# Routed attention and a gated convolution FFN on one core: query pieces of 512 and 256 in place of two of 384, f32 weight loads, and a new order

## The chip, the cores and the metric

The kernel runs on one core of a Trainium2 chip. Its engines work from queues of their own and meet at semaphores: TensorE (PE in the profile; its weight loads are listed as PEld), VectorE (DVE), ScalarE (ACT), GpSimd (POOL) and SyncE (SP), which here only issues transfers (DMA). The metric is device time of one execution in microseconds, the median of several runs.

## The reference

Attention over 4 batches, 8 heads, 768 tokens and head size 64, in which a query sees only the keys that are nearest to the same one of 16 centroids, and then a feed-forward network with a 3-tap depthwise convolution as its gate:

```python
q_assign = np.argmax(np.einsum('bhsd,hcd->bhsc', q_n, c_n), axis=-1)
k_assign = np.argmax(np.einsum('bhsd,hcd->bhsc', k_n, c_n), axis=-1)
mask = q_assign[:, :, :, None] == k_assign[:, :, None, :]
scores = scale * np.matmul(q, k.transpose(0, 1, 3, 2))
scores = np.where(mask, scores, -1000000000.0)
attn = np.exp(scores - np.max(scores, axis=-1, keepdims=True))
attn = attn / (np.sum(attn, axis=-1, keepdims=True) + 1e-09)
x = np.matmul(attn, v)      # heads side by side: (4, 768, 512)

h = np.maximum(x @ w_in, 0.0)               # 512 -> 1024
conv_out = sum(conv_w[k] * hp[:, k:k + S, :] for k in range(3))   # hp: h padded by one
out = h * (1 / (1 + np.exp(-conv_out))) @ w_out                   # 1024 -> 512
```

## The kernel before

Heads are taken two at a time: 16 pairs g, four for each batch. For each pair, queries and keys come in by DMA (`load_q`, `load_k`, or `load_blocks`), are turned so that the head's 64 features lie along the partitions, and are cast to f16 into `ext`. Pairs 0 to 5 are loaded as rows of 64 values and turned by PE (`transposes`, L303, then `chunk_copy`, L316 and L318). Pairs 6 to 15, listed in `BLOCKS`, are loaded in pieces of 32 values by eight transfers a pair (`load_blocks`, L284) and turned by DVE in blocks (`turn_blocks`, L312). Centroid similarities (`assign`, L345), an argmax on DVE (`argmax`, L371 to L402), a turn on PE (`turn`, L407) and a copy (`spk`) give three more rows, 64 to 66, that carry the routing into the product as a bias; one transfer puts them in place (`bias_rows`, L415), and another shifts the second head's rows to partition 0 (`shift_pair`, L332). The pool of loaded pairs, `qk_in`, has three buffers, so pair g+3 can be loaded when pair g has been turned.

Attention runs in 32 slots t, eight for a batch: first the four pairs with queries 0 to 383, then the four with queries 384 to 767. A slot has six steps. In each, PE makes two 128x384 score tiles into one of two PSUM tiles `sc` (`scores`, L440), ACT takes the exponential of both at once (`exps`, L452, 768 columns), and PE multiplies with the values (`values`, L463). A column of ones beside the values gives the sum, by which DVE divides (`normalize`, L476 and L477). The result `x` is turned into `xT`, by PE for slots 0 to 3 and 28 to 31 and by a transposing transfer for the others (`xT_transfer`, L499).

The feed-forward network runs in eight units for each batch: half of the tokens, two blocks of 128 channels. A unit takes eight projection matmuls (`ffn_in`, L518), two relus (`relu`, L531 on ACT or L533 on DVE), three tap steps for each block on DVE (`tap`, L552 and L554; for five units of the last batch PE does the convolution, `conv`, L560), a tanh on ACT (`tanh`, L581) and a gate on DVE (`gate`, L589). Output matmuls (`ffn_out`, L601) gather all units of a batch, and `evac` (L614, L616) and `store` (L619) bring them out. Two or three columns at the seam of the token halves pass through POOL (`carry`, L540 and L542).

Weights are loaded by DMAs that POOL issues and that turn f32 into f16 on the way (`load_weights`, L627 and L632).

Nothing is scheduled by the compiler. `PLAN`, a string of some 1,700 tokens, gives the order in which every step is written; each engine and each DMA queue carries out its own steps in that order. `S.1.0@0` is scores of slot 1, step 0, into `sc` 0; `E`, `V` and `N` are exponential, values and normalising; `T.3.0@3` is the turning of chunk 0 of pair 3 into PSUM bank 3; `LQ`, `LK` and `LV` are loads, `CX` is the row shift, `BX` the bias rows.

Of the kernel before, what the change touches and what calls it, by code (L numbers as in the profile page):

```python
# [20 lines left out]
NHP = 3  # L21
NBH = 1
BLOCKS = (6, 7, 8, 9, 10, 11, 12, 13, 14, 15)

# [822 lines left out]
```

## Time and profile before

| | us |
|---|---|
| median of 3 runs (272.72, 272.73, 276.73) | 272.73 |
| profiled execution, its own time | 274.73 |
| its span, first to last instruction | 272.9 |
| first exponential begins | 15.76 |
| exponentials of slots 8, 16 and 24 begin | 78.78, 139.29, 195.38 |
| last exponential begins | 242.83 |

An idle engine is told with the event that ended its wait. Two views of who waited for whom matter here. The first is for ACT's exponentials and for PE's scores (engine and line, then what it waited for, us in total, times, longest):

```
ACT attn L452 <- PE sc L440: 16.5, 30, 1.9
PE sc L440 <- ACT attn L452: 2.7, 7, 1.2
DVE hg L589 <- ACT th L581: 5.9, 8, 1.7
```

The second is for SP's queue, whose issues stand in one line:

```
SPq L415 <- ACT attn L452: 16.3, 8, 5.1
SPq L332 <- POOL ext L318: 11.6, 3, 7.4
SPq L499 <- DVE cnv L554: 11.0, 5, 5.4
```

A matmul's end is modelled, so a PE that is listed as busy need not run at its peak. The granted clock is given as a share of full speed.

### The profile page before, as it was taken

Reading aid. Unit: us, or ns where it says so; the run is one execution under the profiler, and the core shown is the slowest. Engines: PE = TensorE matmul, PEld = TensorE weight load, DVE = VectorE, ACT = ScalarE, POOL = GpSimd, SP = SyncE. Lnnn points to the kernel's source line nnn. Section 1 sums busy time; section 2 is a strip of 40 time slices with the busy share of each in tenths; the row PEclk is TensorE's granted clock in tenths of the full one; section 3 lists DMA queues with packets and bytes.
Section 4 is the critical chain, followed back from the end, with each engine's and each line's share of the span. In section 5 each row is a group of like instructions: output and inputs, shape, how many; then the busy total and the mean of one; then the engine's idle time right before and its main releaser. Section 6 shows DMA issues by size and latency. Waiting matters only on the chain.

```text
span 272.9 us, 6362 instructions
## 1 busy us (share of the span) xinstructions
PE 243.0 (89%) x2414; PEld 149.0 (55%) x2414; DVE 218.6 (80%) x456; ACT 214.2 (78%) x338; POOL 83.2 (30%) x158
## 2 busy tenths in 40 slices
...
PEclk9999555799999799779999999999999999999999
...
GB/s 185 225 224 218 124 151 175 142 188 109 161 150 158 141 172 148 99 127 73 197 115 121 156 46 147 143 114 52 116 171 4 34 24 123 40 79 0 77 4 154
DMA packets 116458, 33.32 MB, mean 122 GB/s; under 512 B 109320, under 2 KB 111880, under 8 KB 116427
## 3 DMA queue, kind: packets, MB, share of 16 engines
...
q10 hardware_dynamic: 928, 0.23, 0.4%
q14 instruction: 12, 0.10, 0.1%
...
## 4 chain that ended last, share of the span: by engine, by line
DVE 35%; PE 29%; DMA 12%; ACT 9%; issue 5%; SPq 5%; POOL 2%; ACTq 0%; DVEq 0%; POOLq 0%
DVE cnv L554 12%; PE sc L440 9%; DMA qk_in<-in_q_dram 6%; ACT attn L452 5%; DVE qkT L312 4%; DVE hg L589 4%; PE flex L463 4%; PE flex L601 4%; SPq L284 3%; PE sc L601 3%; DVE cnv L552 3%; DMA ext<-ext 2%; ACT th L581 2%; PE flex L303 2%; DVE x L477 2%
## 5 line engine op out<-in xcount | busy, mean ns | idle before, releaser
L452 ACT ACTIVATE attn<-sc 128x768 f16<-128x768 f32 x192 | 148.9, 815 | 17.8 <-PE sc L440 16.5
L440 PE MATMUL sc<-ext 67*128 67x384 f16 x384 | 98.7, 350 | 5.1 <-ACT attn L452 2.7
L554 DVE SCALAR_TENSOR_TENSOR cnv<-hpad,cwcol,cnv 128x382 f16<-128x382 f16 (+1 forms) x108 | 68.2, 641 | 2.5
L463 PEld LDWEIGHTS <-attn 128*128 128x128 f16 x1152 | 52.8, 101 | 21.0 <-issue 7.2
L463 PE MATMUL flex<-v,attn 128*128 128x65 f16 x1152 | 56.9, 198 | 1.9 <-ACT attn L452 1.2
L440 PEld LDWEIGHTS <-ext 67*128 67x128 f16 x384 | 34.5, 103 | 31.1 <-issue 10.6
L318 POOL CAST ext<-qkT 128x768 f16<-128x768 f32 (+1 forms) x28 | 26.5, 960 | 68.1 <-PE sc L440 21.1
L601 PE MATMUL flex<-w_out,hg 128*128 128x512 f16 x152 | 44.1, 389 | 3.3 <-DVE hg L589 1.6
L518 PE MATMUL flex<-xT,w_in 128*128 128x384 f16 x228 | 45.7, 330 | 0.6 <-DVE sim L371 0.6
L589 DVE SCALAR_TENSOR_TENSOR hg<-th,hpad 128x764 f16<-128x764 f32 (+3 forms) x37 | 32.0, 870 | 6.0 <-ACT th L581 5.9
L518 PEld LDWEIGHTS <-w_in 128*128 128x128 f16 x256 | 24.5, 98 | 18.0 <-issue 2.6
L601 PEld LDWEIGHTS <-hg 128*128 128x128 f16 x192 | 17.5, 99 | 22.7 <-issue 7.5
L581 ACT ACTIVATE th<-cnv 128x764 f32<-128x764 f16 (+1 forms) x27 | 22.9, 851 | 7.5 <-DVE cnv L554 7.1
L531 ACT ACTIVATE hpad<-flex 128x384 f16<-128x384 f32 x47 | 22.7, 505 | 3.7 <-PE flex L518 3.6
L312 DVE STREAM_TRANSPOSE qkT<-qk_in 128x384 f32<-128x384 f32 x40 | 21.4, 558 | 1.3 <-DMA qk_in<-in_k_dram 0.8
L552 DVE TENSOR_SCALAR cnv<-hpad,cwcol 128x382 f16<-128x382 f16 (+1 forms) x54 | 18.6, 353 | 1.3 <-ACT hpad L531 1.2
L722 POOL TENSOR_SCALAR taps<-id,cwcol 128x128 f16<-128x128 f16 x24 | 19.4, 821 | 0.0
L477 DVE TENSOR_TENSOR x<-flex,rec 128x384 f16<-128x384 f32 x32 | 17.8, 557 | 1.1
L318 POOL CAST v<-v_in 128x768 f16<-128x768 f32 x14 | 12.4, 891 | 16.0 <-DMA v_in<-in_v_dram 11.0
L303 PE MATMUL flex<-id,qk_in 128*128 128x128 f32 x72 | 14.0, 347 | 2.5 <-ACT cP L681 1.0
L540 POOL COPY hf<-hpad 128x6 f16<-128x6 f16 x16 | 4.8, 303 | 32.6 <-ACT hpad L531 26.6
L542 POOL COPY hpad<-hf 128x6 f16<-128x6 f16 x16 | 5.5, 346 | 28.4 <-DVE hg L589 27.9
...
## 6 DMA issues: line engine op xcount, KB each, us to landing
...
```

Source lines behind the costliest of these rows:

```text
L312: nc.vector.transpose(turned(g)[:, 384 * i : 384 * (i + 1)], src)
L318: (nc.vector if name == "d" else nc.gpsimd).tensor_copy(out=to, in_=src)
L440: nc.tensor.matmul(sc[at][:, n, 0:HS], lhsT=ext_b[g % NE][0:KR, h, 1, P * (kt + n) : P * (kt + n + 1)], rhs=ext_b[g % NE][0:KR, h, 0, HS * ...
L452: nc.scalar.activation(attn[t, i // 3][:, kt : kt + 2, :], sc[at][:, :, 0:HS], AF.Exp, scale=0.125)
L463: nc.tensor.matmul(avp(at)[:, 3 * h + jq, 0 : D + 1], lhsT=attn[t, h][:, kt, P * jq : P * (jq + 1)], rhs=v16_b[g % NE][:, h, kt, 0 : D + 1 ...
L477: nc.vector.tensor_tensor(out=x16[t].rearrange("p jq (h d) -> p h jq d", h=2), in0=av[:, :, 0:D].rearrange("p (h jq) d -> p h jq d", h=2), ...
L518: nc.tensor.matmul(bank[at][:, 0:HS], lhsT=w_in16[:, r, 2 * u + f, :], rhs=xT[:, b % 2, r, HS * a : HS * (a + 1)], start=(r == 0), stop=(r ...
L552: nc.vector.tensor_scalar(out=cnv, in0=src, scalar1=w, scalar2=None, op0=ALU.mult)
L554: nc.vector.scalar_tensor_tensor(out=cnv, in0=src, scalar=w, in1=cnv, op0=ALU.mult, op1=ALU.add)
L581: nc.scalar.activation(to, pre, AF.Tanh, scale=0.5)
L589: nc.vector.scalar_tensor_tensor(out=hg_b[b][:, 2 * u + fs.start : 2 * u + fs.stop, LO[a] : LO[a] + N], in0=th_t[n][:, fs, 0:N], scalar=1. ...
L601: nc.tensor.matmul(bank[at][:, 0:Dm], lhsT=hg_b[b][:, fb, P * tq : P * (tq + 1)], rhs=w_out16[:, fb, :], start=(fb == 0), stop=(fb == NFB ...
```

## The change

Queries of a pair are now taken as 512 and 256. The first four slots of a batch have 512 queries, with two 128x512 tiles to a step, and the last four have 256, with four 128x256 tiles. So a slot has six or three steps of 1024 columns, with one exponential each. Each head of a 512-slot has a PSUM bank of its own for its values and is normalised by itself; the reciprocal is a step of its own (`P`).

The feed-forward network follows: for each batch four units of 512 tokens and two channel blocks, and two units of 256 tokens and four channel blocks. Units 19, 22 and 23 are convolved by PE.

Pairs 6 and 7 leave `BLOCKS` and are loaded and turned as pairs 0 to 5 are. For the pairs that stay, the keys are put in another order when they are cast, so that every pair's values can be loaded by one transfer with runs of 1536 bytes; POOL reads the keys with a step of six for that.

Weights come as f32 over SP into the buffers of `hg` and `th` and are cast by POOL (four), ACT (two) and DVE (two). Convolution weights come as 24 rows of 128 and are turned at once. Twelve matmuls of zeros (`_k`) are put in at the beginning, and `PLAN` is new throughout.

```diff
-BLOCKS = (6, 7, 8, 9, 10, 11, 12, 13, 14, 15)
+BLOCKS = (8, 9, 10, 11, 12, 13, 14, 15)
...
-    "LQ.0.0 _zero _cent _hz.1 _v.0 _cT _v.3 _v.4 _pk.3 LK.0.0 La.0.1 _id LQ.1.0 _n0 _pk.2 _id16 _pk.0 LV.0 "
+    "LQ.0.0 _cent _io _cT _v.1 _id La.0.1 LK.0.0 _zero _pk.1 _id16 _n0 LQ.0.1 _v.0 _v.4 _v.2 _k.0@0 _pk.0 "
...
-    HS = S // 2
-    NU = 2 * NPR
+    NU = NPR + NPR // 2
+    QN = (4 * P, S - 4 * P)
+    Q0 = (0, QN[0])
+    NF = (2, 4)
+    CUT = QN[0] - 2
...
     def cast_pair(name, g, x):
-        copy(name[2:], ext_b[g % NE][:, 0, x], qkT[g][:, x, :])
+        to, src = ext_b[g % NE][:, 0, x], qkT[g][:, x, :]
+        if x and g in BLOCKS:
+            to, src = to.rearrange("p (j t) -> p j t", j=J), src.rearrange("p (t j) -> p j t", j=J)
+        copy(name[2:], to, src)
...
+    def key_tiles(a, i):
+        n = 2 if a == 0 else 4
+        return [divmod(n * i + m, J) for m in range(n)]
...
     def exps(t, i, at):
+        a = slot(t)[1]
         if i % 3 == 0:
-            attn[t, i // 3] = rot.tile([P, J, HS], F16, name="attn", tag="attn", bufs=NAT)
-        kt = 2 * (i % 3)
-        nc.scalar.activation(attn[t, i // 3][:, kt : kt + 2, :], sc[at][:, :, 0:HS], AF.Exp, scale=0.125)
+            attn[t, i // 3] = rot.tile([P, J * QN[0]], F16, name="attn", tag="attn", bufs=NAT)
+        to = attn[t, i // 3][:, 1024 * (i % 3) : 1024 * (i % 3 + 1)]
+        nc.scalar.activation(to, sc[at].rearrange("p n s -> p (n s)"), AF.Exp, scale=0.125)
...
+    def reciprocals(t, h):
+        rec_t[t, h] = rot.tile([P, 4, 1], F32, name="rec", tag="rec")
+        nc.vector.reciprocal(out=rec_t[t, h][:], in_=avp(av_at[t, h])[:, :, D : D + 1])
+    def normalize(t, h):
+        av, rec = avp(av_at[t, h]), rec_t.pop((t, h))
+        if t not in x16:
+            x16[t] = rot.tile([P, 4, P], F16, name="x16", tag="x16", bufs=NX)
+        if slot(t)[1] == 0:
+            to, src, by = x16[t][:, :, D * h : D * (h + 1)], av[:, :, 0:D], rec[:].to_broadcast((P, 4, D))
+        else:
+            to = x16[t][:, 0:2].rearrange("p jq (h d) -> p h jq d", h=2)
...
+        nc.vector.tensor_tensor(out=to, in0=src, in1=by, op=ALU.mult)
...
     def unit(n):
-        return n // NU, n % NU // NPR, n % NPR
+        b, m = divmod(n, NU)
+        a = int(m >= NPR)
+        return b, a, m - NPR * a, NF[a] * (m - NPR * a)
...
-    def load_weights(i):
+    def load_weights(i, queue=nc.sync):
+        if i < 6:
+            if i % 3 == 0:
+                staged = rot.tile([P, NFB, S], F16, name="hg", tag="hg").bitcast(F32)
...
+        else:
+            staged = rot.tile([P, TH], F32, name="th", tag="th")
+            to = stage[i] = staged[:, 0:Dff]
         if i < R:
-            nc.gpsimd.dma_start(
-                w_in16[:, i].rearrange("p fb f -> p (fb f)"), moe_w_in[P * i : P * (i + 1), :]
-            )
+            queue.dma_start(to, moe_w_in[P * i : P * (i + 1), :])
...
+    def cast_weights(name, i):
+        if i < R:
+            to = w_in16[:, i].rearrange("p fb f -> p (fb f)")
+        else:
+            to = w_out16[:, 2 * (i - R) : 2 * (i - R) + 2].rearrange("p f d -> p (f d)")
+        copy(name[2:], to, stage.pop(i))
```

How the steps now stand is seen on three engines. In these rows a name is followed by the number of its buffer: `flex_68` to `flex_71` are PSUM banks 0 to 3, `sc_66` and `sc_67` the two score tiles, `ext_90` to `ext_92` the cast pairs 0 to 2. A row ends with its output's shape.

PE at its start, before:

```order
L670 MATMUL flex_68<-id_72,cn 128x128
L303 MATMUL flex_68<-id_72,qk_in 128x128 x3
L303 MATMUL flex_69<-id_72,qk_in 128x128 x3
L345 MATMUL flex_69<-qkT,cH 32x192 x4
L303 MATMUL flex_69<-id_72,qk_in 128x128 x3
```

and now, from the eleventh of the twelve matmuls of zeros on (`cn` are the centroids, `qk_in` the first pair):

```order
L686 LDWEIGHTS id_73
L686 MATMUL flex_68<-zero,id_73 128x384
L709 MATMUL flex_69<-id_72,cn 128x128
L297 MATMUL flex_70<-id_72,qk_in 128x128 x3
L297 MATMUL flex_71<-id_72,qk_in 128x128 x3
```

Eleven such matmuls stand ahead of the centroids, and the first two chunks of the pair no longer use the centroids' bank.

ACT from the copies of pair 1's chunks on, before:

```order
L316 ACTIVATE qkT<-flex_71 128x512
L316 ACTIVATE qkT<-flex_70 128x512
L452 ACTIVATE attn<-sc_66 128x768
L452 ACTIVATE attn<-sc_67 128x768
L316 ACTIVATE ext_90<-flex_71 3x384
L452 ACTIVATE attn<-sc_66 128x768
L316 ACTIVATE qkT<-flex_70 128x512
L452 ACTIVATE attn<-sc_67 128x768
```

and now:

```order
L310 ACTIVATE qkT<-flex_68 128x512
L310 ACTIVATE ext_91<-qkT 128x768 x2
L310 ACTIVATE ext_90<-flex_71 3x384
L459 ACTIVATE attn<-sc_66 128x1024
L459 ACTIVATE attn<-sc_67 128x1024
L310 ACTIVATE qkT<-flex_71 128x512
L459 ACTIVATE attn<-sc_66 128x1024
L459 ACTIVATE attn<-sc_67 128x1024
```

Both casts of pair 1 (`ext_91`) and the bias rows of pair 0's second head now stand ahead of the first exponential.

SP's queue from the key loads of pair 3 on, before:

```order
L278 DMA qk_in<-in_k_dram 128x6x64 x2
L332 DMA ext_91<-ext_91 64x1536
L706 DMA cw_in<-in_moe_conv_w_dram 3x1024
L291 DMA v_in<-in_v_dram 128x2x384
L274 DMA qk_in<-in_q_dram 128x6x64
L415 DMA ext_91<-spk 3x24x128
```

and now:

```order
L276 DMA qk_in<-in_k_dram 128x6x64 x2
L329 DMA ext_91<-ext_91 64x1536
L272 DMA qk_in<-in_q_dram 128x6x64
L287 DMA v_in<-in_v_dram 128x2x384
L661 DMA hg<-in_moe_w_in_dram 128x1024
L413 DMA ext_91<-spk 3x24x128
```

Pair 3's second query load has moved ahead of a value load, the convolution weights have moved further back, and the first weight load has come in.

More of the change, by code (lines that the diff above doesn't have):

```diff
@@ L245 @@
     pack_b = [const.tile([P, P], F16, name=f"pack{i}") for i in range(NPK)]
-    hpad_b = [[const.tile([P, 2, HW], F16, name=f"hpad{a}_{i}") for i in range(NHP)] for a in range(2)]
+    hpad_b = [
+        [const.tile([P, NF[a], HW[a]], F16, name=f"hpad{a}_{i}") for i in range((NHP, NHQ)[a])] for a in range(2)
+    ]
     qk_t, v_t, qkT, chunk_at = {}, {}, {}, {}
@@ L340, in assign @@
         for x in range(2)[heads(h)]:
-            tokens = qkT[g][:, x].rearrange("p (c j t) -> p j c t", c=J, j=4)
+            by = "p (j t c) -> p j c t" if x and g in BLOCKS else "p (c j t) -> p j c t"
+            tokens = qkT[g][:, x].rearrange(by, c=J, j=4)
             w = cH[:, x] if g < NBH else cP[:, g % NPR]
@@ L425, in rows_copy @@
         at = turn_at[g, h, x]
-        copy(name[2:], ext_b[g % NE][D:KR, h, x, HS * a : HS * (a + 1)], bank16[at][D:KR, HS * a : HS * (a + 1)])
-    attn, x16, x_at, av_at = {}, {}, {}, {}
+        cut = (0, S // 2 if x else QN[0], S)
+        cols = slice(cut[a], cut[a + 1])
+        copy(name[2:], ext_b[g % NE][D:KR, h, x, cols], bank16[at][D:KR, cols])
+    attn, x16, x_at, av_at, rec_t = {}, {}, {}, {}, {}
     def slot(t):
@@ L454, in avp @@
+        to = attn[t, i // 3][:, 1024 * (i % 3) : 1024 * (i % 3 + 1)]
+        nc.scalar.activation(to, sc[at].rearrange("p n s -> p (n s)"), AF.Exp, scale=0.125)
     def avp(at):
[L455 removed]
+        return bank[at][:, 0 : 4 * VW].rearrange("p (u w) -> p u w", u=4)
     def values(t, i, at):
         b, a, pr, g = slot(t)
[L459 to L462 removed]
+        n = QN[a] // P
@@ L463, in values @@
+        av_at[t, i // 3] = at
+        for jq in range(n):
+            for m, (h, kt) in enumerate(key_tiles(a, i)):
+                o = 1024 * (i % 3) + QN[a] * m + P * jq
                 nc.tensor.matmul(
-                    avp(at)[:, 3 * h + jq, 0 : D + 1],
-                    lhsT=attn[t, h][:, kt, P * jq : P * (jq + 1)],
+                    avp(at)[:, jq + (2 * h if a else 0), 0 : D + 1],
+                    lhsT=attn[t, i // 3][:, o : o + P],
                     rhs=v16_b[g % NE][:, h, kt, 0 : D + 1],
-                    start=(i == 0 and jq == 0 and kt == 0),
+                    start=(i % 3 == 0 and jq == 0 and m == 0),
@@ L470, in values @@
                 )
-    def normalize(t):
-        av = avp(av_at[t])
-        rec = rot.tile([P, J, 1], F32, name="rec", tag="rec")
-        x16[t] = rot.tile([P, 3, P], F16, name="x16", tag="x16", bufs=NX)
-        nc.vector.reciprocal(out=rec[:], in_=av[:, :, D : D + 1])
-        nc.vector.tensor_tensor(
-            out=x16[t].rearrange("p jq (h d) -> p h jq d", h=2),
-            in0=av[:, :, 0:D].rearrange("p (h jq) d -> p h jq d", h=2),
-            in1=rec[:].rearrange("p (h jq) o -> p h jq o", h=2).to_broadcast((P, 2, 3, D)),
-            op=ALU.mult,
-        )
-        del attn[t, 0], attn[t, 1]
+    def reciprocals(t, h):
[9 more added lines that the diff above has]
+            to = x16[t][:, 0:2].rearrange("p jq (h d) -> p h jq d", h=2)
+            src = av[:, :, 0:D].rearrange("p (h jq) d -> p h jq d", h=2)
+            by = rec[:].rearrange("p (h jq) o -> p h jq o", h=2).to_broadcast((P, 2, 2, D))
+        nc.vector.tensor_tensor(out=to, in0=src, in1=by, op=ALU.mult)
+        del attn[t, h]
     def x_transposes(t, at):
         x_at[t] = at
-        for jq in range(3):
+        for jq in range(QN[slot(t)[1]] // P):
             nc.tensor.transpose(bank16[at][:, P * jq : P * (jq + 1)], x16[t][:, jq, :], id16[:])
@@ L491, in xT_of @@
         b, a, pr, g = slot(t)
-        return xT[:, b % 2, pr, HS * a : HS * (a + 1)]
+        return xT[:, b % 2, pr, Q0[a] : Q0[a] + QN[a]]
     def xT_copy(name, t):
-        copy(name[1:], xT_of(t), bank16[x_at[t]][:, 0:HS])
+        copy(name[1:], xT_of(t), bank16[x_at[t]][:, 0 : QN[slot(t)[1]]])
         del x16[t]
     def xT_transfer(t):
+        n = QN[slot(t)[1]] // P
         nc.sync.dma_start(
-            xT_of(t).rearrange("p (j s) -> p j s", j=3), x16.pop(t).rearrange("p j c -> p (j c)"), transpose=True
+            xT_of(t).rearrange("p (j s) -> p j s", j=n),
+            x16.pop(t)[:, 0:n].rearrange("p j c -> p (j c)"),
+            transpose=True,
         )
```

148 lines of the change are left out of this document (76 added, 72 removed), and 275 rows, old and new, of the table PLAN.

## Prediction

> **What bounds the kernel now.** I read the page first, then busy time by stage, the start in order of time, and the groups with their shapes kept apart. The page's head:
>
> ```profile
> span 272.9 us, 6362 instructions
> PE 243.0 (89%) x2414; PEld 149.0 (55%) x2414; DVE 218.6 (80%) x456; ACT 214.2 (78%) x338; POOL 83.2 (30%) x158
> PEclk9999555799999799779999999999999999999999
> ```
>
> PE looks fullest, but its 243.0 us hold a stretch at half clock, so DVE and ACT are as near to being the bound. The windows below are cut where the exponentials of slot 0, slot 4 and slots 8, 16 and 24 (batches 1 to 3) begin and where the last one ends. The columns are length, busy time and number of PE, weight loads, DVE, ACT and POOL, then granted clock, DMA share and GB/s.
>
> ```profile
> 0.00:15.76 15.76, 8.47 (x57) 5.93 (x57) 8.01 (x29) 8.58 (x16) 3.11 (x30) 1.00 1.01 218
> 15.76:52.24 36.48, 32.83 (x302) 22.65 (x300) 17.91 (x43) 23.76 (x34) 9.91 (x14) 0.67 0.90 168
> 52.24:78.78 26.54, 25.02 (x303) 16.17 (x300) 25.38 (x53) 24.77 (x40) 13.51 (x21) 1.00 0.93 143
> 78.78:139.29 60.51, 53.96 (x547) 31.63 (x544) 54.56 (x107) 50.13 (x81) 17.70 (x29) 0.92 0.92 142
> 139.29:195.38 56.09, 53.15 (x587) 31.96 (x586) 54.49 (x113) 51.23 (x81) 16.41 (x28) 1.00 0.54 111
> 195.38:243.64 48.26, 47.31 (x512) 29.35 (x509) 43.43 (x90) 44.83 (x67) 16.13 (x28) 1.00 0.23 73
> 243.64:272.90 29.26, 22.21 (x131) 11.29 (x127) 14.79 (x27) 10.93 (x23) 6.40 (x10) 1.00 0.15 55
> ```
>
> From 52 to 195 us DVE is the bound: 134.4 of 143.1 us. It idles 7.8 us before the first exponential, 18.6 us in slots 0 to 3, then 1.2, 6.0, 1.6 and 4.8 us, and 14.5 us in the tail, where PE has more to do. These sum to 54.3 us beside 218.6 us of work. That makes the second row the place to win something. Its reason:
>
> ```profile
> 6.16 1.54 PE L303 MATMUL flex<-id,qk_in 128*128 128x128 f32 x6 [1.00 <-ACT cP L681]
> 13.69 1.70 PE L303 MATMUL flex<-id,qk_in 128*128 128x128 f32 x12
> 20.28 7.60 DMA qk_in<-in_q_dram
> 28.01 1.94 PE L303 MATMUL flex<-id,qk_in 128*128 128x128 f32 x8 [0.94 <-DMA qk_in<-in_q_dram]
> 27.75:51.65 23.90, 23.64 (x175) 16.30 (x176) 6.23 (x14) 15.79 (x22) 5.07 (x8) 0.50 0.86 152
> ```
>
> A turning transpose takes 1.54/6 = 257 ns at 6 us, 1.70/12 = 142 ns at 13.7 us and 242 ns at 28 us: PE starts slow although the window prints 1.00, runs fast, and is slow again after pair 3's queries, issued at 20.28, kept it waiting 7.60 us. For 23.90 us it is then busy all the time at half clock, with ACT at 15.79 and DVE at 6.23 us. The third rate is what this stretch costs.
>
> **The change by parts.** Prices come from these groups (operation, shapes, count, busy time, mean ns):
>
> ```profile
> L452 ACT ACTIVATE attn<-sc 128x768 f16<-128x768 f32 x192 | 148.9, 815 | 17.8 <-PE sc L440 16.5
> L316 ACT ACTIVATE qkT<-flex 128x512 f32<-128x512 f32 x11 | 6.2, 598 | 3.4 <-PE flex L303 3.4
> L316 ACT ACTIVATE qkT<-flex 128x384 f32<-128x384 f32 x3 | 1.5, 491 | 1.9 <-PE flex L303 1.6
> L318 DVE COPY qkT<-flex 128x512 f32<-128x512 f32 x4 | 2.8, 692 | 6.5 <-PE flex L303 6.5
> L318 DVE COPY qkT<-flex 128x384 f32<-128x384 f32 x1 | 0.6, 557 | 1.3 <-PE flex L303 1.3
> L318 DVE CAST ext<-qkT 128x768 f16<-128x768 f32 x2 | 1.3, 629 | 0.0
> L318 DVE COPY spk<-flex 72x128 f16<-72x128 f16 x3 | 0.6, 204 | 0.0
> L312 DVE STREAM_TRANSPOSE qkT<-qk_in 128x384 f32<-128x384 f32 x40 | 21.4, 558 | 1.3 <-DMA qk_in<-in_k_dram 0.8 <-issue 0.5
> L477 DVE TENSOR_TENSOR x<-flex,rec 128x384 f16<-128x384 f32 x32 | 17.8, 557 | 1.1
> L476 DVE RECIPROCAL rec<-flex 128x6 f32<-128x6 f32 x32 | 5.9, 183 | 8.8 <-PE flex L463 8.8
> L554 DVE SCALAR_TENSOR_TENSOR cnv<-hpad,cwcol,cnv 128x382 f16<-128x382 f16 x60 | 38.5, 650 | 1.4
> L554 DVE SCALAR_TENSOR_TENSOR cnv<-hpad,cwcol,cnv 128x386 f16<-128x386 f16 x48 | 29.7, 630 | 1.1
> L552 DVE TENSOR_SCALAR cnv<-hpad,cwcol 128x382 f16<-128x382 f16 x30 | 10.8, 364 | 1.3 <-ACT hpad L531 1.2
> L552 DVE TENSOR_SCALAR cnv<-hpad,cwcol 128x386 f16<-128x386 f16 x24 | 7.7, 340 | 0.0
> L589 DVE SCALAR_TENSOR_TENSOR hg<-th,hpad 128x764 f16<-128x764 f32 x15 | 14.7, 981 | 0.7 <-ACT th L581 0.7
> L589 DVE SCALAR_TENSOR_TENSOR hg<-th,hpad 128x386 f16<-128x386 f32 x8 | 4.3, 557 | 2.8 <-ACT th L581 2.8
> L533 DVE TENSOR_SCALAR hpad<-flex 128x384 f16<-128x384 f32 x10 | 5.4, 553 | 1.6 <-PE flex L518 1.4
> L616 DVE TENSOR_SCALAR o_sb<-flex 128x512 f32<-128x512 f32 x7 | 4.8, 686 | 1.1 <-PE flex L601 0.9
> L531 ACT ACTIVATE hpad<-flex 128x384 f16<-128x384 f32 x47 | 22.7, 505 | 3.7 <-PE flex L518 3.6
> L394 DVE TENSOR_SCALAR pack<-best 128x24 f16<-128x24 f32 x4 | 0.7, 176 | 0.1
> L318 POOL CAST ext<-qkT 128x768 f16<-128x768 f32 x27 | 25.4, 954 | 62.5 <-PE sc L440 21.1 <-DVE qkT L318 13.2 <-DVE qkT L312 9.3
> ```
>
> *Exponentials.* 192 of 768 columns become 144 of 1024. One costs 148.9/192 = 0.775 us of ACT; ACT's slope is (598-491)/128 = 0.84 ns a column, so 0.775+0.215 = 0.99 us and 142.6 us in all, 6.3 us less. Bounds are no gain (time per column kept, 1.033 us each) and -37 us (0.775 us kept). I take the slope, from the nearest rows. 52 relus of 384 (505 ns) become 40 of 512 (near 598 ns), -2.3 us, and six spk copies go to DVE; with two weight casts and two other casts and two final copies added, ACT falls by about 6 us. Since DVE is fuller, this alone shortens nothing after slot 4; it counts in slots 0 to 3.
>
> *Score, value and projection matmuls* stay 384, 1152 and 256, with the same columns: 0.
>
> *Normalising.* 32 pairs become 48, of 256 columns. By the copies' slope, (692-557)/128 = 1.05 ns, one multiply costs 557-135 = 422 ns, between 371 (two thirds) and 557 (no shorter): 48 x (422+183) = 29.0 against 23.7 us, DVE +5.3 (+2.9 to +11.8).
>
> *Ten pairs' blocks to eight.* Eight block transposes go: 8 x 0.535 = -4.3 us of DVE. Pairs 6 and 7 are turned by PE, and Qd copies rise from 5 to 13: +7 x 0.692 +0.557 = +5.4. PE gets 24 more transposes at 142 ns, 3.4 us, where it has slack or costs little.
>
> *Convolution, gates, relus.* The gates' slope is (981-557)/378 = 1.12 ns. 60 tap steps grow from 642 to 785 ns, 48 shrink from 619 to 476: +1.7; the first taps, at 364 and 340 ns, get half that slope: +0.4, at most +1. Gates go from 37 to 31 instructions at equal columns: -0.6. DVE relus go from 12 x 0.553 to 8 x 0.692: -1.1. Widths below every row are the weak point here.
>
> *Weights* come over SP as f32 and are cast: four casts on POOL, two on ACT, two on DVE. The DVE ones cost 4/3 of 629 ns each, +1.7. On POOL they stand ahead of pair 3's casts, and so of its row shift; their loads are issued well ahead, and POOL is 30% busy, so I take 0; were POOL to wait, slot 3's scores would wait next.
>
> *The rest of DVE.* Casts of pair 0 and its values that leave it for ACT and POOL (four of at most 629 ns, -2.3), six more spk copies of 204 ns (+1.2), nine packing steps taken over from POOL (+1.6, at 176 ns or less), two fewer final copies (-1.4, at 686) and xT copies (+0.5). Altogether DVE grows by some 8 us, to 226.
>
> *Warm-up and order.* Twelve dummy matmuls fill PE's wait for the centroids: at 6 us a transpose should be near 142 ns, about 1.5 us less on the first chain. Against this, ACT now casts pair 1 before the first exponential, which I put at 18 us instead of 15.76. Pair 3's last query load stands on SP directly behind the first row shift, ahead of the convolution weights and pair 2's values. I expect it some 3 us earlier, and PE to have 512-wide scores in hand, so that PE is not drained at 24-28 us and stays at full clock.
>
> [...]
>
> **The sum.** I added the DVE rows between the same marks of each kernel's order, scaled by what the windows show of before (0.90 to 1.01 of the row means). DVE gets 9 us before the first exponential (before 8.0), 24 in slots 0 to 3 (17.9), 24 in slots 4 to 7 (25.4), 49, 52 and 48 in batches 1, 2 and 3 (54.6, 54.5, 43.4) and 19.5 in the tail (14.8): 225.5. Its idle time: 9 at the start; 7 in slots 0 to 3, whose ACT work (27.5 us) sets the length at 31; 1.5, 3.5, 1.6 and 4 in the dense stages, about as now except where batch 1 loses six of its DVE us; 12.5 in the tail, 3 us longer for more PE and DVE work. That is 39 us, and 225.5+39 = 265 us. The profiled execution took 274.73 us for its span of 272.9; the median of the runs shown is 272.73, so I take the span's scale for the median: 265.
>
> **The rivals.**
> *The clock still drops (0.20).* PE again waits for pair 3 or 4 and slots 0 to 3 keep their 18.6 us of DVE idle: 265+11 = 276, less what wider work fills in, 272 to 278. For it: nothing warms PE at 20-28 us. Against it: the load's earlier place.
> *DVE grows more than its slopes say (0.08), ending slower.* If narrow pieces keep the old price (48 x 135 ns of normalising, 48 x 143 ns of taps, 24 first taps at 70 ns), DVE gets 15 us more; batches 1 to 3 and the tail have no cover, so 13 of them show: 278, reaching 284. It decides from about 13 us on, that is if the 256-wide multiply stays near 557 ns and the 258-wide tap near 630.
> *POOL's casts hold DVE up (0.10).* Eight pairs' keys are now read with a step of six. In these rows the same DVE tap takes 0.32 us alone and 0.88 us beside POOL casts:
>
> ```profile
> 107.16 0.32 DVE L552 TENSOR_SCALAR cnv<-hpad,cwcol 128x386 f16<-128x386 f16 x1
> 108.48 1.79 POOL L318 CAST ext<-qkT 128x768 f16<-128x768 f32 x2 [5.00 <-PE sc L440]
> 108.71 0.88 DVE L552 TENSOR_SCALAR cnv<-hpad,cwcol 128x386 f16<-128x386 f16 x1
> ```
>
> If a stepped cast took twice 954 ns, 7.6 us more of POOL would stall DVE for at least the share that the taps and gates of the rows above have of it (106 of 218.6 us): 3.7 us, 267 to 271. [...] No run here shows such a read.
> *Better than this (0.07).* ACT fills slots 0 to 3 without idling and the tail keeps its length: 252 to 258.
>
> **Numbers.** The forecast itself has 0.55, with 259 to 271 as its own range. A measurement of this kernel tells 2% from no change, 267.3 to 278.2 us. Below lie four fifths of the forecast (0.44), the better case (0.07) and a quarter of POOL's (0.03): 0.54. Above lies the DVE rival with a sliver of the clock's: 0.08. The rest, 0.38, is within. Between 257 and 275 I leave out DVE's rival, the upper quarter of the clock's and a little below: under 0.2. It also takes in both ends of the normalising price (-2.4, +6.5).
>
> **What will show it.** The clock at 28 to 52 us; the first exponential near 18 us and batch 1's near 74, batch 2's near 127, batch 3's near 181, the last one's end near 233; DVE near 226 us; the exponential at 0.99 us; 422 ns for the multiply; POOL's stepped cast near 954 ns. I am wrong if DVE is under 95% busy between 75 and 180 us, for then something else is late, most likely a row shift or a load.

## The result and the profile after

| | before | after |
|---|---|---|
| median, us | 273.23 (4 runs) | 256.39 (254.91 to 257.54, 4 runs) |
| ratio after/before, 95% interval | | 0.9355, 0.9259 to 0.9452 |
| profiled execution, its own time | 274.73 | 257.09 |

The gain is 16.8 us; 8 were forecast, and 256.39 lies just under the range of 257 to 275. First the head of the page and the granted clock in 40 slices:

```profile
span 255.3 us, 6344 instructions
PE 233.6 (92%) x2443; PEld 144.1 (56%) x2443; DVE 219.2 (86%) x490; ACT 208.8 (82%) x269; POOL 89.2 (35%) x138
PEclk9999999979997999999999999989999999999998
```

DVE's busy time did not grow: 219.2 against 218.6 us. The long half clock of slots 0 to 3 is gone. The windows are cut at the same exponentials as before (columns: length; busy time and number of PE, weight loads, DVE, ACT and POOL; clock, DMA share, GB/s):

```profile
0.00:18.02 18.02, 12.80 (x101) 7.74 (x101) 10.04 (x32) 10.26 (x19) 5.20 (x32) 1.00 1.01 210
18.02:50.33 32.31, 27.86 (x373) 18.71 (x372) 24.41 (x62) 26.67 (x31) 13.16 (x17) 1.00 0.89 248
50.33:73.39 23.06, 20.97 (x213) 14.07 (x214) 19.97 (x40) 21.14 (x31) 6.18 (x11) 0.93 0.88 174
73.39:122.05 48.66, 46.98 (x525) 27.83 (x524) 47.58 (x107) 43.16 (x53) 19.95 (x25) 0.96 0.84 143
122.05:176.42 54.37, 51.35 (x574) 31.49 (x570) 52.08 (x118) 47.48 (x60) 19.45 (x21) 0.97 0.63 132
176.42:225.65 49.23, 49.18 (x518) 30.57 (x515) 47.48 (x104) 47.66 (x60) 15.78 (x21) 1.00 0.22 63
225.65:255.30 29.65, 24.47 (x158) 13.66 (x154) 17.61 (x33) 12.44 (x24) 9.48 (x14) 0.97 0.21 80
```

Against the forecast, in us (idle is length less DVE busy):

| stage | length forecast, measured | DVE busy forecast, measured | DVE idle forecast, measured |
|---|---|---|---|
| to the first exponential | 18, 18.0 | 9, 10.0 | 9, 8.0 |
| slots 0 to 3 | 31, 32.3 | 24, 24.4 | 7, 7.9 |
| slots 4 to 7 | 25.5, 23.1 | 24, 20.0 | 1.5, 3.1 |
| batch 1 | 52.5, 48.7 | 49, 47.6 | 3.5, 1.1 |
| batch 2 | 53.6, 54.4 | 52, 52.1 | 1.6, 2.3 |
| batch 3 | 52, 49.2 | 48, 47.5 | 4, 1.8 |
| tail | 32, 29.7 | 19.5, 17.6 | 12.5, 12.0 |
| sum | 264.6, 255.3 | 225.5, 219.2 | 39, 36.1 |

Of the 9.3 us between forecast and result, 6.3 are DVE work that did not come and 3.0 are idle time. The prices of the wider and narrower pieces were not the reason, as the groups show (count, busy us, mean ns):

```profile
L459 ACT ACTIVATE attn<-sc 128x1024 f16<-128x1024 f32 x144 | 141.0, 1034 | 9.3 <-PE sc L445 8.4
L579 DVE SCALAR_TENSOR_TENSOR cnv<-hpad,cwcol,cnv 128x510 f16<-128x510 f16 x60 | 45.3, 780 | 0.1
L579 DVE SCALAR_TENSOR_TENSOR cnv<-hpad,cwcol,cnv 128x258 f16<-128x258 f16 x48 | 23.7, 525 | 0.0
L495 DVE TENSOR_TENSOR x<-flex,rec 128x256 f16<-128x256 f32 x48 | 19.7, 413 | 0.5
L483 DVE RECIPROCAL rec<-flex 128x4 f32<-128x4 f32 x48 | 8.0, 169 | 3.9 <-PE flex L472 3.9
L312 POOL CAST ext<-qkT 128x768 f16<-128x768 f32 x27 | 32.3, 1214 | 34.0 <-PE sc L445 18.5 <-ACT qkT L310 8.6 <-DVE qkT L306 5.0
```

An exponential takes 141.0/144 = 0.98 us (forecast 0.99), the multiply 413 ns (422), the long tap 780 (785). The short tap, at 525 ns (476), adds 2.4 us and takes none away. What differs is how the rows stand beside each other. Here are DVE's rows in order of time (start, duration), before:

```profile
105.31 0.16 DVE L476 RECIPROCAL rec<-flex 128x6 f32<-128x6 f32 x1
105.50 0.56 DVE L477 TENSOR_TENSOR x<-flex,rec 128x384 f16<-128x384 f32 x1
105.98 1.27 DVE L554 SCALAR_TENSOR_TENSOR cnv<-hpad,cwcol,cnv 128x386 f16<-128x386 f16 x2
```

and after:

```profile
115.61 0.17 DVE L483 RECIPROCAL rec<-flex 128x4 f32<-128x4 f32 x1
115.72 0.55 DVE L385 TENSOR_REDUCE best<-val 128x24 f32<-128x384 f16 x1
116.19 0.41 DVE L495 TENSOR_TENSOR x<-flex,rec 128x256 f16<-128x256 f32 x1
116.52 0.62 DVE L392 TENSOR_SCALAR pack<-best 128x24 f16<-128x24 f32 x1
```

Before, the multiply reads the reciprocal just ahead of it and starts 0.03 us after that one's end (105.47); the tap behind it reads neither and starts 0.08 us before the multiply's end (106.06). After, a step of another chain stands between, and every row starts 0.06 to 0.08 us before the end of the one ahead. Counted over all neighbouring DVE records of the traces, the gaps fall into two heaps, near -80 and near +35 ns, 115 ns apart: 233 and 168 of them before, 384 and 47 after. By the tiles' names, 158 of the late ones before and 40 after read what their neighbour wrote.

Added up, count times mean over all groups, DVE's records grew from 237.4 to 250.0 us, by 12.6 where 8 were forecast. Busy time counts a moment in which two records overlap once: that is 18.8 us before and 30.8 us after, so the overlap took 12.0 back. By stage, 4.0 of the missing 6.3 us lie in slots 4 to 7, mostly because DVE had run ahead there: 94 of its records begin before slot 4's first exponential, and 88 stand ahead of it in the order. Slots 0 to 7 together have 44.4 us for a forecast of 48, and the overlap in them grew from 3.1 to 5.4 us.

### The profile page after: what moved, and what is told of

The parts are those of the page before. It is cut to its first block, busy times and chain, and to the rows that moved or that the text cites. A ratio compares the mean times of both kernels' runs of the same rounds, so it can differ in the third digit from the quotient of the medians.

```text
span 255.3 us, 6344 instructions
## 1 busy us (share of the span) xinstructions
PE 233.6 (92%) x2443; PEld 144.1 (56%) x2443; DVE 219.2 (86%) x490; ACT 208.8 (82%) x269; POOL 89.2 (35%) x138
## 4 chain that ended last, share of the span: by engine, by line
PE 51%; DVE 27%; DMA 8%; ACT 6%; issue 5%; SPq 2%; POOL 0%; DVEq 0%; POOLq 0%; ACTq 0%
PE sc L445 12%; PE flex L622 11%; PE flex L539 9%; PE flex L472 7%; DVE cnv L579 7%; DMA hg<-in_moe_w_out_dram 4%; PE sc L622 3%; DVE qkT L306 3%; DVE x L495 3%; DMA qk_in<-in_q_dram 3%; DVE hg L610 3%; ACT attn L459 2%; PE flex L297 2%; PE flex L343 2%; PE sc L539 2%
## 5 line engine op out<-in xcount | busy, mean ns | idle before, releaser
L459 ACT ACTIVATE attn<-sc 128x1024 f16<-128x1024 f32 x144 | 141.0, 1034 | 9.3 <-PE sc L445 8.4
L445 PE MATMUL sc<-ext 67*128 67x256 f16 (+1 forms) x384 | 83.7, 329 | 1.8 <-DMA ext<-spk 1.0
L579 DVE SCALAR_TENSOR_TENSOR cnv<-hpad,cwcol,cnv 128x510 f16<-128x510 f16 (+1 forms) x108 | 68.8, 667 | 0.1
L472 PEld LDWEIGHTS <-attn 128*128 128x128 f16 x1152 | 47.4, 98 | 23.1 <-ACT attn L459 6.2
L539 PE MATMUL flex<-xT,w_in 128*128 128x512 f16 (+1 forms) x220 | 44.7, 341 | 0.4 <-ACT th L602 0.2
L610 DVE SCALAR_TENSOR_TENSOR hg<-th,hpad 128x1020 f16<-128x1020 f32 (+3 forms) x31 | 32.6, 1066 | 3.4 <-ACT th L602 3.3
L602 ACT ACTIVATE th<-cnv 128x1020 f32<-128x1020 f16 (+1 forms) x21 | 22.6, 1075 | 3.7 <-DVE rec L483 2.3
L553 ACT ACTIVATE hpad<-flex 128x512 f16<-128x512 f32 x34 | 20.0, 622 | 5.1 <-PE flex L539 4.4
L495 DVE TENSOR_TENSOR x<-flex,rec 128x256 f16<-128x256 f32 x48 | 19.7, 413 | 0.5
L577 DVE TENSOR_SCALAR cnv<-hpad,cwcol 128x510 f16<-128x510 f16 (+1 forms) x54 | 17.6, 345 | 2.4 <-ACT hpad L553 1.9
L306 DVE STREAM_TRANSPOSE qkT<-qk_in 128x384 f32<-128x384 f32 x32 | 17.6, 557 | 0.9 <-issue 0.9
L343 PE MATMUL flex<-qkT,cP 128*32 128x192 f32 x240 | 15.7, 382 | 0.8 <-DVE x L495 0.5
```

The lines of the kernel that those rows point to most:

```text
L306: nc.vector.transpose(turned(g)[:, 384 * i : 384 * (i + 1)], src)
L343: nc.tensor.matmul(bank[at][32 * j : 32 * (j + 1), o : o + 192], lhsT=w, rhs=tokens[:, j], start=True, stop=True, skip_group_check=True,)
L445: nc.tensor.matmul(to[:, m], lhsT=ext_b[g % NE][0:KR, h, 1, P * kt : P * (kt + 1)], rhs=ext_b[g % NE][0:KR, h, 0, Q0[a] : Q0[a] + QN[a]], ...
L459: nc.scalar.activation(to, sc[at].rearrange("p n s -> p (n s)"), AF.Exp, scale=0.125)
L472: nc.tensor.matmul(avp(at)[:, jq + (2 * h if a else 0), 0 : D + 1], lhsT=attn[t, i // 3][:, o : o + P], rhs=v16_b[g % NE][:, h, kt, 0 : D ...
L495: nc.vector.tensor_tensor(out=to, in0=src, in1=by, op=ALU.mult)
```

## The experiments

Theory 1: the order gained by parting DVE steps that read their neighbour's result. Rivals: 2, the clock and pair 3's load; 3, transfers; 4, the share of work that each stage gets by the new widths and the new order as a whole; 5, POOL's stepped casts, as a loss. Ratios are to the kernel before on the same chip; differences between kernels are differences of ratios times 273 us.

**The neighbours, in the kernel before.** Steps are moved by one or two places; a sample (`P` is the reciprocal, which stood inside `N` before):

```diff
-E.12.3@1 N.11 E.12.4@0 G.6 S.12.5@1
+E.12.3@1 P.11 E.12.4@0 G.6 N.11 S.12.5@1
-c.4.0 LZ.10.1.3 a.4.0 S.10.5@1 Fa.0.0 I.5.0@1 b.4.0 LZ.11.0.0 E.10.5@1 M2.8
+c.4.0 LZ.10.1.3 S.10.5@1 Fa.0.0 I.5.0@1 LZ.11.0.0 E.10.5@1 M2.8 a.4.0 c.4.1 b.4.0
```

> The kernel before with nothing changed but the places of some DVE steps in the order: the reciprocal is a step of its own, and reciprocals, tap steps and argmax steps are moved past one or two neighbours so that a step seldom stands directly behind the one whose result it reads. By the order 155 such neighbours become 48. Theory 1 (a DVE instruction that reads its neighbour's result starts about 35 ns after that one's end, one that doesn't starts about 80 ns before it, so 115 ns a pair): DVE busy falls by about 107 x 0.115 = 12 us from 218.6, and the time by 6 to 11 us, to 262 to 267. Theory 2 (what the change won came from the clock and the start, or from wider pieces): DVE busy within 2 us of 218.6 and the time within 2 us of before.

Measured: ratio 0.9968 (0.9925 to 1.001), 59 late gaps for 168. The chain of work that ended last in the kernel before, by engine:

```profile
DVE 35%; PE 29%; DMA 12%; ACT 9%; issue 5%; SPq 5%; POOL 2%; ACTq 0%; DVEq 0%; POOLq 0%
```

and in this one, with the head of its page:

```profile
PE 238.9 (88%) x2414; PEld 146.9 (54%) x2414; DVE 210.7 (78%) x456; ACT 213.5 (79%) x338; POOL 81.2 (30%) x158
...
PE 40%; DVE 19%; DMA 15%; ACT 13%; SPq 7%; issue 4%; POOL 1%; ACTq 0%; DVEq 0%
```

DVE lost 7.9 us of busy time where 12 were expected, 0.07 us for each of 109 gaps: of the 115 ns only the 80 of overlap are busy time, the other 35 were idle. The time stayed almost the same: the chain's share of DVE fell to 19% and PE's rose to 40%. Theory 1 is right in kind on DVE and wrong on the time of this kernel.

**Pair 3's load and the clock, in the kernel before.** Alone, and with the edit above:

```diff
-LK.3.0 S.0.0@0
+LK.3.0 LQ.3.1 S.0.0@0
...
-M3.1 Qa.2.2 LQ.3.1 S.0.5@1
+M3.1 Qa.2.2 S.0.5@1
```

> The kernel before with pair 3's second query load issued directly behind its other loads, ahead of the first row shift, of the convolution weights and of pair 2's values. Theory 2 (the late load drains PE and so the clock): no half clock from 28 to 52 us, DVE idles less in slots 0 to 3, 266 to 269. Theory 1 has nothing to say on the clock. Rival: PE waited 2.15 us for the argmax of pair 2 just ahead of this load (0.94 us), and that wait alone drops the clock: then the half clock stays and the time is within 1 us of before.

> The kernel before with both edits, the separated DVE steps and pair 3's early query load; widths, loads, weights, casts and all sizes are those of before. Theory 1 with theory 2 as a second and smaller part: 257 to 263, most of what the whole change won. If the wider pieces and the other loads made the gain: 268 or more.

Measured: 0.9999 (0.9967 to 1.003) and 0.9973 (0.9933 to 1.0012). With the early load alone the half clock in slots 0 to 3 shrank from 23.9 us to two stretches of 3.4 and 6.8 us, and these slots from 36.5 to 34.1 us:

```profile
15.75:49.83 34.08, 27.41 (x302) 19.26 (x301) 17.73 (x44) 23.19 (x35) 9.77 (x14) 0.85 0.95 176
```

That is half of theory 2. The first stretch begins at 27.6 us as before, behind a wait of PE's of 2.17 us that the load has no part in. In the kernel before this wait was for the last step of pair 2's argmax, just ahead of the 0.94 us for the load:

```profile
26.84 0.23 PE L407 MATMUL flex<-id,pack 128*128 128x128 f16 x1 [2.15 <-DVE pack L402]
```

That fits the rival named beforehand, that this wait alone drops the clock, for the 3.4 us behind it; what began the stretch of 6.8 us was not shown. The median did not move, and with both edits the time is on the rivals' side ("268 or more").

**The neighbours, in the changed kernel.** First crudely (all three taps at the last one's place), then on the places where the steps stood:

```diff
-c.3.0 O.0.0.0@1 LZ.9.1.0 c.3.1 E.8.1@1 a.3.0 V.8.0@2 LZ.10.0.0 S.8.2@0 a.3.1
+c.3.0 O.0.0.0@1 LZ.9.1.0 a.3.0 E.8.1@1 b.3.0 V.8.0@2 LZ.10.0.0 S.8.2@0 c.3.1
```

> The changed kernel with every reciprocal put directly ahead of its multiply and the three tap steps of a block put one behind the other at the place of the last. By the order 38 DVE steps that read their neighbour's result become 190. Theory 1: DVE busy rises by 152 x 0.115 = 17 us from 219.2, and the time by 10 to 17 us, to 266 to 274. Theory 2: DVE busy within 2 us of 219.2 and the time within 2 us of the changed kernel, 254 to 259.

> The changed kernel with every reciprocal directly ahead of its multiply, and with the tap steps of two blocks one block after the other on the very places where they stood mixed, so that no step of the pair ends later by the order. 38 DVE steps that read their neighbour's result become 106. Theory 1: DVE busy rises by 68 x 0.115 = 7.8 us from 219.2 and the time by 4 to 9 us, to 260 to 266; then most of the 22 us of the cruder run is this, and some is its later places. If DVE's busy time rises and the time stays at 255 to 258, the neighbours are no cause of the gain in the changed kernel either.

Measured: 1.019 (1.0125 to 1.0256) with 200 late gaps, and 0.949 (0.9446 to 0.9533) with 117. The crude run lost 22.8 us, more than 153 gaps of 115 ns; its page has DVE at

```profile
PE 237.7 (86%) x2443; PEld 144.6 (52%) x2443; DVE 232.5 (84%) x490; ACT 209.7 (76%) x269; POOL 87.8 (32%) x138
```

13.3 us more than the changed kernel, and 9 us more idle (45.1 against 36.1): the taps' later places cost too. The clean one lost 3.7 us for 70 gaps, 0.05 us each, just under its expectation; DVE was busy for 222.8 us, 3.6 more where 7.8 were expected. Its interval touches that of the changed kernel (0.9446 to 0.9452), and its profile has 17.1 us of half clock where the changed kernel's has 10.2, so a price in time is suggested and not shown. At 0.05 us each the 121 gaps between the two kernels would be some 6 us, an estimate.

**Parting what is left.** 25 more steps moved apart in the changed kernel:

> The changed kernel with only those 25 DVE steps moved apart. Theory 1: DVE busy 2 to 3 us less, time 254 to 256 (1 to 2 us less than the changed kernel on the same chip). If the order as it stands is the bound: no change or slower.

Measured: 0.9384 (0.9323 to 0.9446), no gain, with DVE at 217.7 us and 24 fewer late gaps. As in the kernel before, DVE was busy for less (1.5 us less here, 7.9 there) and the time was not clearly shorter.

**Transfers.** The block loads read the same bytes in runs of 3072:

```diff
-src = (k if x else q)[b, h0 + r // 2, :, 32 * (r % 2) : 32 * (r % 2 + 1)]
-nc.sync.dma_start(to, src.rearrange("(n t) d -> t n d", t=32))
+src = (k if x else q)[b, h0 + r // 2, 384 * (r % 2) : 384 * (r % 2 + 1), :]
+nc.sync.dma_start(to, src.rearrange("(p j) d -> p (j d)", j=12))
```

> The kernel before, but the 80 block loads of pairs 6 to 15 read the same bytes in runs of 3072 bytes in place of 128 (so the queries and keys of these pairs are not the reference's rows; sizes, order and every other instruction are the same). Theory 3 (DMA, whose engines are 0.90 to 1.01 busy up to 139 us before, is what the other engines wait for there, and the change's fewer and longer pieces relieve it): DMA share in batch 1 falls from 0.92 to under 0.7, slots 4 to 7 and batch 1 together (87 us) shrink by 5 to 10 us, the time is 262 to 268. Theory 4 (the order written for the old durations holds the engines to its own pace, whatever one of them could gain): the time stays within 2 us of before.

> The kernel before with all three: separated DVE steps, pair 3's early query load, and the long runs of the block loads. Theory 3: with DVE and DMA both relieved the gain is larger than that of either, 255 to 262. Theory 4: 268 or more, though no engine is over 90% busy and DMA is relieved.

> The changed kernel with the 64 block loads of pairs 8 to 15 in runs of 3072 bytes in place of 128 (queries and keys of these pairs are not the reference's rows). Theory 3, if DMA still bounds the changed kernel up to the end of batch 1: 248 to 253. If the change took DMA off the path: within 2 us of the changed kernel, 254 to 259.

Measured: 0.987 (0.9786 to 0.9955), 0.9819 (0.9739 to 0.9898) and 0.935 (0.9282 to 0.9418). In the kernel before, crowded transfers cost some 3.6 us (theory 3 gave 5 to 10), most of it in batch 1 (57.5 for 60.5 us), where DMA's share fell to 0.58. With all three edits it is 4.9 us: not the larger gain of theory 3 (255 to 262 us), but theory 4's "268 or more". In the changed kernel the long runs made no difference that can be told from noise.

**POOL's casts and the loads of pairs 6 and 7.** First both edits of the loads undone, then only the stepped cast, with the values in short runs that it was made for; then that with 25 neighbours parted:

```diff
-        if x and g in BLOCKS:
-            to, src = to.rearrange("p (j t) -> p j t", j=J), src.rearrange("p (t j) -> p j t", j=J)
...
+        if g in BLOCKS:
+            for h in range(2):
+                queue.dma_start(v_t[g][:, h], v[b, h0 + h].rearrange("(j p) d -> p j d", p=P))
```

> The changed kernel with its two edits of the loads undone: pairs 6 and 7 are again loaded in pieces of 32 values and turned by DVE, and the values of pairs 6 to 15 are loaded head by head in runs of 256 bytes, with the keys cast in their own order. POOL's casts go back to 0.95 us, DVE gains some 1 us of work. Theory 3: batch 1 grows by 3 us or more, the time is 260 to 266. Theory 4 or DVE alone: 256 to 260.

> The changed kernel with the keys of pairs 8 to 15 cast in their own order again, so that POOL reads without a step, and for that the values of these pairs loaded head by head in runs of 256 bytes. Nothing else is touched. Theory 5 (POOL's stepped casts hold DVE up: in the kernel with the loads undone DVE was busy for 214.0 us against 219.2, though it turned 8 more blocks): DVE busy falls by 6 to 9 us, batches 1 and 2 get 4 us shorter, 250 to 254. Theory 3 (short runs of DMA cost more than that): 257 to 262. If the two cancel, 254 to 257.

> The kernel of the run with the plain casts, and 25 more of the DVE steps that read their neighbour's result moved apart (38 by the order become 13). Theory 1 prices that at 25 x 0.115 = 2.9 us of DVE busy, and where DVE is the bound (batches 1 to 3) 1 to 2 us of time: 249 to 252. If DVE no longer binds once POOL lets go of it: the same as with the plain casts alone.

Measured: 0.944 (0.9371 to 0.951), 0.9104 (0.9019 to 0.9189) and 0.9262 (0.9189 to 0.9336). With plain casts the median is 250.77 us, the fastest kernel here. Its page:

```profile
span 248.9 us, 6353 instructions
PE 227.2 (91%) x2443; PEld 142.8 (57%) x2443; DVE 213.7 (86%) x490; ACT 208.1 (84%) x269; POOL 84.8 (34%) x138
```

its cast and one of the gates, which took 1455 ns in the changed kernel, and, from the changed kernel's trace in order of time, one of the stepped casts:

```profile
L306 POOL CAST ext<-qkT 128x768 f16<-128x768 f32 x27 | 26.8, 1009 | 39.0 <-PE sc L437 21.0 <-ACT qkT L304 8.5 <-DVE qkT L300 6.4
L602 DVE SCALAR_TENSOR_TENSOR hg<-th,hpad 128x1032 f16<-128x1032 f32 x6 | 7.3, 1220 | 0.0
105.45 1.57 POOL L312 CAST ext<-qkT 128x768 f16<-128x768 f32 x1
```

Eight of the 27 casts were stepped: 32.3-26.8 = 5.5 us of POOL. In the trace they take 1.57 to 1.75 us, one of them 2.98; the shortest plain cast takes 0.82. DVE, at the same instructions, was busy 5.5 us longer beside them, just under the 6 to 9 expected, and the records added up are 5.3 us longer (250.0 against 244.7). So the changed kernel lost 6.9 us by its stepped keys, net of what the longer runs of the values saved, and theory 5 holds. Most of it is batch 2's (49.4 for 54.4 us). The clock is not the reason: executions of the changed kernel at a granted clock of 0.99 took 254.91 and 255.69 us, those with plain casts at 0.99 and 1.00 took 250.74 and 250.79.

The first run, with both edits undone, stays in the range of "theory 4 or DVE alone", and batch 1 did not grow (48.8 us). But the way back to ten pairs' blocks costs 9.2 us on top of the plain casts. 6.4 of them fall into slots 4 to 7, with plain casts

```profile
49.40:72.76 23.36, 19.45 (x213) 13.63 (x214) 21.51 (x41) 21.05 (x30) 8.59 (x11) 1.00 0.94 185
```

and with the blocks of pairs 6 and 7:

```profile
50.04:79.84 29.80, 18.17 (x191) 11.25 (x190) 25.55 (x53) 19.03 (x26) 9.02 (x14) 0.86 0.96 149
```

DVE has 4 us more to do in this stage, though not in the whole kernel (214.0 against 213.7 us), and the clock is lower; whether the work, the clock or the later landing of short pieces sets its length was not separated. Parting neighbours on top of the plain casts was 4.3 us slower, with an interval that touches theirs: PE fell to half clock at 20.9 us and slots 0 to 3 took 33.95 us in place of 31.73.

**The warm-up, and the late load, in the changed kernel.**

The first leaves out `_k.0` to `_k.11`; the second moves one load:

```diff
-BBd.0.1.0.0 BBd.0.1.0.1 LQ.3.1 Qd.2.0
+BBd.0.1.0.0 BBd.0.1.0.1 Qd.2.0
...
-V.0.3@3 BX.1 E.0.4@0
+V.0.3@3 BX.1 LQ.3.1 E.0.4@0
```

> The changed kernel without the twelve matmuls of zeros. If they only speed the first chunks of pair 0 up: the transposes of pair 0 take some 250 in place of 217 and 147 ns, the first exponential comes 0.5 to 1.5 us later, time up by 0 to 1.5 us. If they also keep the clock up later on: a half-clock stretch appears between 20 and 60 us and the time rises by 2 to 6 us.

> The changed kernel with pair 3's second query load issued behind the bias rows of pair 1, some 5 us later, so that PE waits for it as in the kernel before. By the prediction's step: half clock appears between 25 and 50 us and slots 0 to 3 grow by 3 to 6 us, the time is 259 to 263. By what the early load did in the kernel before (clock 0.85 in place of 0.67 in slots 0 to 3, the time the same): within 2 us of the changed kernel.

Measured: 0.9425 (0.9337 to 0.9513), 1.9 us and not clear, with the first exponential at 19.07 in place of 18.02 us and full clock from 16.0 to 53.6 us (with the warm-up from 7.8 to 52.2); and 0.9557 (0.9494 to 0.9619), 5.5 us. In the second, PE waits, then turns slowly, and slots 0 to 3 grow by 4.7 us at a clock of 0.86. The load was issued at 24.51 us; PE's first rows behind the wait, in order of time (start, duration, in brackets the wait, for which the profile names no releaser):

```profile
27.16 1.09 PE L287 MATMUL flex<-id,qk_in 128*128 128x128 f32 x4 [3.22 <-issue]
28.04 1.06 PE L435 MATMUL sc<-ext 67*128 67x512 f16 x2
```

and the stage:

```profile
17.68:54.72 37.04, 31.39 (x373) 21.09 (x372) 23.50 (x61) 26.79 (x31) 13.35 (x17) 0.86 0.75 213
```

Four transposes take 1.09 us there, 272 ns each; the half clock begins inside the wait, at 25.5 us. So a late load costs in this kernel what the prediction said of it; the warm-up is not what keeps the clock.

**The weights**, loaded as before the change, on top of the plain casts:

```diff
-            queue.dma_start(to, moe_w_in[P * i : P * (i + 1), :])
+            nc.gpsimd.dma_start(
+                w_in16[:, i].rearrange("p fb f -> p (fb f)"), moe_w_in[P * i : P * (i + 1), :]
+            )
```

> The kernel of the run with the plain casts, and its weights loaded as before the change, by transfers that POOL issues and that turn f32 into f16, without the eight casts. If the new way of the weights brought something: 253 to 256, against 250.8 with the plain casts alone. If it only cost its casts (2.0 us of DVE, 4.2 us of POOL, two ACT casts): 248 to 251.

Measured: 0.9321 (0.9273 to 0.9368), 5.9 us more, though DVE had 2.2 us less to do. All of it lies in slots 0 to 3 (37.15 us for 31.73), where loads moved 187 in place of 244 GB/s and the clock fell from 1.00 to 0.91. So the new way of the weights pays here, by slots 0 to 3; how much of that is the transfers and how much the clock behind them was not separated.

**All of it in the kernel before.** Pairs 6 and 7 by rows and PE; then with separated steps and the early load:

```diff
-BLOCKS = (6, 7, 8, 9, 10, 11, 12, 13, 14, 15)
+BLOCKS = (8, 9, 10, 11, 12, 13, 14, 15)
...
-        n = 384 if g < NBH else 512
+        n = 384 if g < NBH or g in (6, 7) else 512
...
-CCp.6.1 Ra.3.1 BX.4 Z.7.0 S.6.4@0 E.6.3@1
+CCp.6.1 T.7.0@1 Ra.3.1 BX.4 S.6.4@0 T.7.1@3 Qd.7.0 E.6.3@1
```

> The kernel before with pairs 6 and 7 loaded as rows and turned by PE in four chunks of 384 columns, which DVE copies at the places of its block turns, and their values loaded by one transfer each; DVE's work is the same to 0.1 us. In the changed kernel the return to ten pairs' blocks cost 8.3 us (259.1 against 250.8). Theory 3 (the loads of these pairs are the cause): 264 to 268. If the order before already hid them: 271 to 274.

> The kernel before with all edits that could be made without its new widths and its new order: separated DVE steps, pair 3's early query load, pairs 6 and 7 by rows. If these make the gain between them: 255 to 262. Theory 4 (the share of the work that each stage gets, by 512 and 256 queries and by the new order, makes it): 266 or more.

Measured: 1.0018 (0.9988 to 1.0049) and 0.998 (0.9949 to 1.0012): nothing. With all of it DVE was at 210.3 us and DMA's share in slots 4 to 7 at 0.75 for 0.93 (in batch 1 at 0.86 for 0.92), and the time was the same.

**Room in slots 0 to 3.** A third score matmul and a second exponential in each of the 24 steps:

```diff
+        if t < 4:
+            nc.scalar.activation(attn[t, i // 3][:, kt, 0:256], sc[at][:, 0, 0:256], AF.Exp, scale=0.125)
```

> The kernel before with work added in slots 0 to 3 alone, about what a width of 512 in place of 384 queries would add there: in each of their 24 steps a third 128x384 score matmul (a repeat of the second) and a second exponential of 256 of the same columns, some 24 x 0.16 = 4 us of PE and 24 x 0.35 = 8 us of ACT. Theory 4 in its first part (what sets the length of slots 0 to 3 is the loading and routing of pairs 1 to 4, in whose shadow wider slots cost nothing, so that 512 queries there take work off slots 4 to 7): slots 0 to 3 stay within 2 us of 36.5 and the time within 2 us of before. If attention itself sets their length: 4 to 8 us more.

Measured: 1.0314 (1.0228 to 1.0401), 8.6 us slower; the stage

```profile
16.50:58.60 42.10, 39.73 (x321) 25.44 (x319) 17.57 (x40) 32.71 (x58) 9.68 (x14) 0.65 0.80 140
```

grew by 5.6 us, with PE busy 39.73 of 42.10 at a clock of 0.65. There was no free room in the kernel before, at least not at its clock; this part of theory 4 falls.

## Why the prediction missed

- *DVE's work, 225.5 us: the term that was mis-sized; it measured 219.2.* The step "I added the DVE rows between the same marks of each kernel's order, scaled by what the windows show of before (0.90 to 1.01 of the row means)" took the overlap of neighbours as a constant of the engine. It is a matter of the order: moving steps alone took 7.9 us off DVE in the kernel before. The rows themselves were forecast well: the prediction has them grow by 8 us, and with plain casts they grew by 7.3 (237.4 to 244.7). The stall beside the stepped casts made that 12.6, and the overlap, whose share the prediction kept, took back 12.0: at 80 ns each the 121 late gaps that went are 9.7 of it, and the rest fits the 34 steps more.
- *POOL's stepped cast, taken at 954 ns.* It was 1.57 us or more, and the rival "POOL's casts hold DVE up" was real: 5.5 us of DVE where the rival was priced at 3.7, and 6.9 us of time. The error above hid it, by the opposite sign: in batches 1 to 3 DVE was busy for 147.1 us of a forecast of 149, with plain casts for 140.2. That DVE's work there came out near the forecast is luck. The shortest stepped cast took 1.57 us, nearly twice the 0.82 us of the shortest plain one. The quarter of this rival's chance that was put below 267.3 us rests on no run; the runs showed 6.9 us of time lost with the stepped casts.
- *"From 52 to 195 us DVE is the bound."* Too strong. With 5.7 us of DVE work taken out of these stages of the kernel before, they got 1.5 us shorter (141.6 for 143.1), and PE got the largest share of the chain.
- *The clock.* The long half clock went, slots 0 to 3 took 32.3 us (forecast 31), and bringing the load back late cost 5.5 us. That fits in the changed kernel; in the kernel before the early load gained nothing, which the prediction would not have said. Its reading of that stretch was off: the 7.60 us are the load's own time from issue to landing, and PE waited 0.94 us for it, behind 2.15 us for the argmax.
- *Idle time.* Batches 1 and 3 idle 4.7 us less than forecast, slots 4 to 7 1.6 us more. Batch 3 has PE busy 49.18 of 49.23 us: that PE sets the end there fits the chain of the whole kernel (PE 51%, DVE 27%). The share of busy time alone does not show it: in the kernel before PE was listed as busy for 23.64 of 23.90 us at a clock of 0.50.
- *The warm-up.* The first six transposes took 217 ns, the next six 147 (forecast: near 142), and it brought 1.05 us of the 1.5.
- *Right:* the first exponential (18.0), batch 2 (54.4), the prices of exponential and multiply, DVE over 95% busy in batches 1 and 2 (47.6 of 48.7 and 52.1 of 54.4), in part by the stall. *"Better than this"* named the time (252 to 258) with half of its reason: the tail kept its length, but ACT idles 5.6 us in slots 0 to 3.

What stays open: three parts of the change (neighbours, early load, pairs 6 and 7 by rows) gain nothing in the kernel before, each and together (0.998), while in the changed kernel taking one out costs 3.7 (neighbours, not clear of noise), 5.5 (early load) and, on the plain casts, 9.2 (blocks) and 5.9 us (weights). These sum to more than the gain of 16.8 us, so they can't be its shares: an undo in a fixed order also counts what a rewritten order would win back. That the parts pay only in an order written around them fits this and was not tested. How the rest is shared between the widths of 512 and 256 and the new order was not separated; the one run on it (more work in slots 0 to 3) spoke against a free place there.
